# S4 convolution with a gated feed-forward block: the last stage's block loads, one transfer over 128 partitions where there were two over 64

## The chip, the cores and the metric

The kernel runs on one core of one Trainium2 chip. The core has a matrix engine (TensorE, PE in the profile, with its weight loads shown as PEld), three engines for elementwise work (VectorE or DVE, ScalarE or ACT, GpSimd or POOL), a queue that only issues transfers (SyncE, SP) and 16 DMA engines that all the queues share. The metric is the device time of one execution in microseconds. Three runs of the kernel before gave 588.81, 591.67 and 594.80 us.

## What is computed

With L = 2048 tokens, D = 512 channels, N = 128 states per channel and F = 1792 hidden units, all in float32:

```python
x  = A_u                                   # [1, 2048, 512]
xn = layernorm(x)
# s: a long convolution along the tokens, one kernel per channel
P  = exp(dt * A * l)                       # A = A_re + i A_im, l = 0..2047
K  = einsum("dn,dnl,dn->dl", C, P, dt * B).real
s  = irfft(rfft(pad(xn)) * rfft(pad(K)))[:L] + xn * Dskip
# z: a gated feed-forward block
z  = (silu(xn @ w_gate) * (xn @ w_up)) @ w_down
out = x + s * silu(z)
```

## The kernel before

The program is one long list of small tasks. Each call of `add` (L154) makes a task: an engine, a few instructions, the buffers that it reads and writes. `Plan.run` (L190) then emits the tasks in an order that is written out by hand: `LIST` (L46 to L84) is a string in which two characters, base 90, give the number of one task in the order of its making. An engine executes its own tasks strictly in that order. `PLACES` gives each SBUF buffer its place in one tile, the `arena`, so most groups of the profile have the name `arena`; a buffer can be filled when the buffers that lay on its place before are done with. PSUM has eight banks, which `run` hands out (L219 to L226): a product needs its banks free.

Transfers are issued by SP and, for a few of the stores, by ACT. In the program as compiled, the transfers of both queues take eight semaphores in turn, and each one waits, before it is issued, for the transfer eight before it in the program to have landed. A transfer that is issued late on ACT so holds back later ones on SP.

The convolution is done with a transform of three stages over token tiles; the feed-forward block runs on PE in between. The work around the change, in the order of the data:

- `s2_mm`, `s2_prod` (L1282, L1307): for each frequency block n = 0 to 7 and each column half c = 0, 1 (256 channels) PE makes the two products (L1294, L1302) into PSUM banks, DVE multiplies them (L1320, L1322), and POOL combines them into the buffer `y` (L1324, L1325).
- `s2_inv` (L1332): for a pair of blocks m = 0 to 3, PE's inverse product (L1347, 64 matmuls) reads the two `y` and fills four banks. ACT (L1357) and DVE (L1355, L1356) empty each bank into a buffer, and SP stores it to the scratch tensor `bs_d` in DRAM (L1359). `bs_d` has the shape [2, 16, 262, 256]: column half, bank of the inverse product (4m + q), row, column. The stores of the two halves are the keys `bs0` and `bs1`.
- `final(b)` (L1362), for the pairs of token tiles b = 0 to 7: the buffer `bt` (8 KB in each of 128 partitions) takes the blocks from `bs_d`; partitions 0 to 63 hold half 0, partitions 64 to 127 half 1, and e = 0, 1 are the two sets of rows. SP also loads the input `x` in four pieces (L1376, buffer `fx`), and the gate silu(z) from the scratch `zg_d` where it was put there (L1379, pairs 0 to 4). DVE adds the sets (L1386), POOL subtracts them (L1389; DVE for the last pair), PE does the last product (L1401) into two banks, DVE multiplies with the gate (L1418), POOL adds `x` (L1419), and SP and ACT store the output in two pieces each (L1421). The last pair, b = 7, has smaller pieces (L1409, L1410, L1412).
- The feed-forward block runs on beside this until the end: products with `w_gate` and `w_up` (L739, 24 matmuls each), products with `w_down` (`down`, L770: L782, 6 matmuls each; L791 for the last tile), the gate's silu on ACT (L761), L763, L765 and L766 on DVE and ACT, and the silu of the result on ACT (L808 and L803).

The last stage's loads are issued by `load` (L466), so that their issues carry the line L467.

Of the kernel before, what the change touches and what calls it, by code (L numbers as in the profile page):

```python
# [19 lines left out]
P = 128  # L20
L = 2048
D = 512
N = 128
# [15 lines left out]
BN = 2 * P + 6  # L39
# [32 lines left out]
    "3V3N4O3X4v,-,/,05D3Z3U3^4:3O3Y3_3g3e3[3f3i,&3`3b3d,14=4@3a,7,84D55,'473]3c3h3j4F,257,3,44N4P4Q3k4w4E4S4B4R4T3l3m"  # L72
    "3p4V4X3n3q3o3r4x4U4W4Z,(5B4G4I5E4H4K5G5F4y4z4{4Y585:4k4i4J4M594L,),*4|5%5#5$4},+3t3s,?565',@5H5I5K4[4]4c4f5&5J4l"
    "4`,95L5M4m4n4j4^4d4g4a4o4q4p6r6t6u4r5],A6v7#4s5N4u4b,:,;,B4e4_635;5?7%6(5>7&7',N4h,<4t5(5=5<5i645/5051525@53545_"
    "5a5)5*5,5-,O,V5`5A5O,C,D6'5P5Q5+5V5.8<5W655X5R5S5T5Y5Z5[5j6667,H8;688:,J8O6<#*6:698N6;6s,I8M8=6=5k5m,K,L,M6)6*,W"
    "6>6,6+605l6.6-,X6/61,Y5n5p5r5o5q,Z,[6w6{6y5U,P626x,],^5s6?6z6}8P6L6F6G6M,Q5t6@6A6I5^6|7_7$6H7[,i,p6J,q6B6C6D6E5b"
    "5e5f5d5c,R,S,T7(7*7`7+,x6N5g7)7,5h8(6K8)6X,_6P7-,U6Q6O6T6U6R,`6S6W7q7^6Y7r5u6$5v7]6Z6[6]6%7o7W6&5w5x7p5|5},y6#,g"
    "7.6^6a8'6b6`6_6V8*7X-%-&7s5y5z6c5{7/7374797:-',h8s757;7677787071,z726d6e6o6p6q6f6l6i,a6g6h,j,c,l6m,k6n6j6k7l877k"
    ",b,d,e,f7m-(7n7t7u7Z89,r,s,t,m7Y7a,u8&-)8#7v-*,n,o,{8%8$887b7c868+7D7w8,8-7A-+8K8?8@7C8o8L8>-.,|7x8J-C,v8I7F7d7y"
    "7=-,7B--8n7e7f8.8]7h80,}7>8A8C8/7K8q8Q8R7{8p,w7i8^-#-$-/7@7<8[-0-18B8D-2-3-6-4-57G-7818S8U8_7?7z7E7}8F-8-:7J-E-9"  # L80
    "8v8w8x7H8T8V7j-;-<7g7M8E8r7N8t-=8`7L->-?8u838d-@-B7I8a9$7|8X7O8b847Q-A8y8c85828e8W9%8z8|-G8G9'-I-K-M8Z9&9)8H9(7P"
    "8f8h7R7V7S8Y9#-D-F7U8}-O-H-Q7T8g8i8l-J-L8k-N-P8j8m9*8{9+9,9.-R90919-949/939295"
)
LIST = [DIGITS.index(a) * 90 + DIGITS.index(b) for a, b in zip(LIST[::2], LIST[1::2])]  # L84
PLACES = (
# [48 lines left out]
class Plan:  # L134
# [19 lines left out]
    def add(self, eng, dur, fn, rd=(), wr=(), up=(), pr=0.0, c=5, dma=0.0, root=False, port=None, f32=0, slack=0.0, ahead=None):  # L154

        t = Task()  # L160
        t.eng, t.dur, t.fn, t.pr, t.due, t.root, t.seq, t.dma = eng, dur, fn, (c, pr), pr, root, len(self.tasks), dma
        t.after = None
        t.f32, t.slack, t.ahead = f32, slack, W["ah"] if ahead is None else ahead
        t.port = eng == "POOL" if port is None else port
        deps = set()
        for b in rd:
            deps.update(b.full)
            deps.update(b.part)
        for b in up:
            deps.update(b.full)  # L170
            deps.update(b.reads)
        for b in wr:
            deps.update(b.full)
            deps.update(b.part)
            deps.update(b.reads)
        for b in rd:
            b.reads.append(t)
        for b in up:
            b.part.append(t)
        for b in wr:  # L180
            b.full.append(t)
        t.bufs = list(dict.fromkeys(b for b in (*rd, *wr, *up) if b.kind))
        for b in t.bufs:
            b.left += 1
        t.deps = deps
        t.succ = []
        self.tasks.append(t)
        return t
# [118 lines left out]
def dma_us(size, pieces):  # L307
    return max(size / 265e3, pieces * 1.3e-3)
# [73 lines left out]
def kernel(  # L382
# [8 lines left out]
    V, S, G, T = nc.vector, nc.scalar, nc.gpsimd, nc.tensor  # L391
# [10 lines left out]
    def pair(a):  # L402
        return a.rearrange("p (k d) -> p k d", k=2)
# [45 lines left out]
    def buf(name, size, group=None, cap=None):  # L449
        b = pl.buf(name, size, group, cap)  # L450
        bufs.append(b)
        return b
# [6 lines left out]
    K = {}  # L459

    def key(name):
        if name not in K:
            K[name] = pl.key(name)
        return K[name]

    def load(dst, src, names, size, pieces, pr, rd=(), ahead=None):  # L466
        add("SP", 0.52, lambda: sy.dma_start(dst(), src), up=names, rd=rd, pr=pr, dma=dma_us(size, pieces), root=True, ahead=ahead)  # L467
# [859 lines left out]
    def bs_rows(c, n, row, pattern):  # L1327

        v = bs_d[c, n, row]
        return bass.AP(tensor=v.tensor, offset=v.offset, ap=[[a * HD, b] for a, b in pattern] + [[1, HD]])  # L1330
# [31 lines left out]
    def final(b):  # L1362

        j0 = 2 * b
        pr = W["o0"] + W["oc"] + W["o1"] * b
        last = b == NB - 1
        bt = buf(f"bt{j0}", 8192, "bt", int(W["c_bt"] + 0.5))
        btv = lambda: bt.f32().rearrange("p (e s d) -> p e s d", e=2, d=HD)
        for h in range(2):
            for e in range(2):  # L1370
                for first, lo, n in ((0, 0, 1), (33, 1, 1), (2, 2, 2)) if b == 0 else ((2 * j0, 0, 4),):
                    load(lambda h=h, e=e, lo=lo, n=n: btv()[h * 64:(h + 1) * 64, e, lo:lo + n], bs_rows(h, 0, e * P + first, ((BN, 16), (32, 4), (1, n))),
                         [bt], 65536 * n, 64, pr, rd=[key(f"bs{h}")])
        fx = buf(f"fx{j0}", 4096, "fx", int(W["c_fx"] + 0.5))
        for g in range(4):
            add("SP", 0.6, lambda g=g: sy.dma_start(pair(fx.f32()[g * 32:(g + 1) * 32]), rows(xv, b, g)), up=[fx], pr=pr, dma=0.6, root=True)  # L1376
        if b < ZK:
            z = buf(f"fz{j0}", 4096, "fz", int(W["c_fz"] + 0.5))
            load(lambda: pair(z.f32()), zg_d.rearrange("j p d -> p j d")[:, j0:j0 + 2], [z], 524288, 256, pr, rd=[key(f"zgd{j}") for j in (j0, j0 + 1)])  # L1379
        elif not last:  # L1380
            z = zgs[b]
        ev = buf(f"ev{j0}", 4096, "ev", 2)
        od = key(f"od{j0}")

        def even():
            V.tensor_tensor(ev.f32(), bt.f32()[:, 0:1024], bt.f32()[:, 1024:2048], op=ALU.add)  # L1386

        def odd():
            E.tensor_tensor(bt.f32()[:, 0:1024], bt.f32()[:, 0:1024], bt.f32()[:, 1024:2048], op=ALU.subtract)  # L1389
        add("DVE", 1.2, even, rd=[bt], wr=[ev], c=1, pr=pr, port=True)  # L1390
        E = V if last else G
        add("DVE" if last else "POOL", 1.2 if last else 2.05, odd, wr=[bt, od], rd=[ev], c=1, pr=pr, port=True)
        py = [bank(f"py{j0}{h}") for h in range(2)]

        def mm():
            src = [ev.f32().rearrange("p (s d) -> p s d", d=HD), btv()[:, 0]]
            for k in range(2):
                for g, (m, _) in enumerate(at(b)):
                    for h in range(2):
                        r = slice(h * 64, h * 64 + 64)  # L1400
                        T.matmul(py[h].t[g * 32:(g + 1) * 32, k * HD:(k + 1) * HD], j2_t[r, (2 * m + k) * 32:(2 * m + k + 1) * 32], src[k][r, 2 * (g % 2) + m],  # L1401
                                 start=True, stop=True, tile_position=(h * 64, g * 32))
        add("PE", 0.92, mm, rd=[bt, ev, key("j2")], wr=py, c=2, pr=pr, f32=6)
        cols = lambda h: slice(h * HD, (h + 1) * HD)
        if last:
            for k in range(2):
                for h in range(2):
                    o, f = zgs[j0 + k][h], (lambda k=k, h=h: pair(fx.f32())[:, k, cols(h)])
                    add("DVE", 0.42, lambda k=k, h=h, o=o: V.tensor_tensor(o.f32(), py[h].t[:, k * HD:(k + 1) * HD], o.f32(), op=ALU.mult), rd=[py[h]], wr=[o], c=1, pr=pr + 5 * k)  # L1409
                    add("DVE", 0.42, lambda o=o, f=f: V.tensor_tensor(o.f32(), o.f32(), f(), op=ALU.add), rd=[fx], wr=[o], c=1, pr=pr + 5 * k, port=True)  # L1410
                    for g in range(4):
                        add(("SP", "ACT")[g % 2], 0.55, lambda g=g, k=k, h=h, o=o: (sy, nc.scalar)[g % 2].dma_start(rows(ov, b, g)[:, k, cols(h)], o.f32()[g * 32:(g + 1) * 32]),  # L1412
                            rd=[o], up=[key("out")], c=0, dma=0.13, pr=pr + 5 * k)
            return
        zh = {h: key(f"zh{j0}{h}") for h in range(2)}
        for h in range(2):
            zv = lambda h=h: pair(z.f32())[:, :, cols(h)]
            add("DVE", 0.7, lambda h=h, zv=zv: V.tensor_tensor(zv(), py[h].t.rearrange("p (k d) -> p k d", k=2), zv(), op=ALU.mult), rd=[py[h], z], wr=[zh[h]], c=1, pr=pr)  # L1418
        add("POOL", 2.05, lambda: G.tensor_tensor(z.f32(), z.f32(), fx.f32(), op=ALU.add), rd=[fx, zh[0], zh[1]], wr=[z], c=1, pr=pr)  # L1419
        for g in range(4):  # L1420
            add(("SP", "ACT")[g % 2], 0.6, lambda g=g: (sy, nc.scalar)[g % 2].dma_start(rows(ov, b, g), pair(z.f32()[g * 32:(g + 1) * 32])), rd=[z], up=[key("out")], c=0,  # L1421
                dma=0.5, pr=pr)
# [55 lines left out]
    for pos, (b, c) in enumerate(seq):  # L1478
        while pos >= lead(pos) and 2 * NB * NC - len(downs) < 2 * (pos - lead(pos)) + 2:
            d = downs.pop(0)  # L1480
# [18 lines left out]
    for b in range(NB):  # L1499
        final(b)  # L1500
# [13 lines left out]
    for t in order:  # L1514
        n = len(made())
# [35 lines left out]
```

## Time and profile before

| | us |
|---|---|
| median of three runs (588.81 to 594.80) | 591.67 |
| time of the profiled execution | 592.23 |
| its span, from the first to the last instruction | 590.3 |
| PE busy | 563.2 |
| DVE busy | 449.4 |
| POOL busy | 343.4 |
| ACT busy | 332.9 |

The profiled execution's time is 1.93 us more than its span, and 0.56 us above the median. Times in the prediction count from the start of the span unless they are called a run's time. A row of a timeline or of the chain of waits has its start, its length, then engine, line, operation, what it writes and reads, how often, and in brackets the engine's idle time before it with what ended it. A row of "windows" has a stretch, its length, the busy time of PE, PEld, DVE, ACT and POOL with their instructions, then the granted clock of PE, the mean busy share of the DMA engines, and the rate of the transfers.

### The profile page before, as it was taken

To read this page: it belongs to the slowest core of one execution; us is meant where nothing else is said; L and a number is where in the kernel's file an instruction comes from. 1 tells how busy PE (TensorE), PEld (TensorE's weight loads), DVE (VectorE), ACT (ScalarE), POOL (GpSimd) and SP (SyncE) were. 2 spreads that over 40 slices of the span, in tenths; PEclk is the share of its full clock that TensorE was granted. 3 is DMA by queue.
4 is the path that set the end of the run, shared out by engine and by line. 5 is a ranking of instruction groups with operands and counts; after the bars stand their busy time and mean duration, and the time that the engine had idled before them with its cause. 6 is when DMAs were issued, how large, how long until landed. Compare 5 with 4: busy or idle time off the path is not lost.

```text
span 590.3 us, 18770 instructions
## 1 busy us (share of the span) xinstructions
PE 563.2 (95%) x7799; PEld 401.0 (68%) x7799; DVE 449.4 (76%) x1004; ACT 332.9 (56%) x686; POOL 343.4 (58%) x303
## 2 busy tenths in 40 slices
PE   8999999999999999999999999999999999999971
PEld 3888875558884787748866688746755664786541
DVE  7998899467889478899688989778788676548451
ACT  5997786457267367769477778746543412311100
POOL 0154621789279777739976999887163145137541
PEclk9999999999999999999999999999999999999996
DMA  8987722331050143076226474298899889997865
GB/s 237 280 271 273 221 98 40 92 125 38 20 90 2 56 81 100 13 155 211 38 74 108 145 144 74 75 164 263 277 220 290 256 262 256 284 221 203 217 194 157
DMA packets 108373, 93.33 MB, mean 158 GB/s; under 512 B 51520, under 2 KB 88256, under 8 KB 108288
## 3 DMA queue, kind: packets, MB, share of 16 engines
q1 hardware_dynamic: 106480, 89.74, 56.5%
q10 hardware_dynamic: 1808, 2.39, 1.6%
q8 instruction: 61, 1.00, 0.7%
q14 instruction: 24, 0.20, 0.1%
HBM read 56.07 MB, written 32.90 MB: 151 GB/s over the span
## 4 chain that ended last, share of the span: by engine, by line
PE 84%; DMA 9%; SPq 3%; issue 2%; DVE 1%; ACTq 0%; ACT 0%; POOL 0%; DVEq 0%; POOLq 0%
PE p L739 45%; PE p L782 22%; PE p L1208 5%; PE p L1294 3%; DMA out_dram<-arena 3%; PE p L1347 2%; DMA wd<-in_B_w_gate_dram 2%; DMA arena<-zg_d 2%; PE p L1302 2%; PE p L576 2%; PE p L1241 1%; DMA arena<-bs_d 1%; SPq L467 1%; DMA arena<-in_A_u_dram 1%; SPq L494 1%
## 5 line engine op out<-in xcount | busy, mean ns | idle before, releaser
L739 PE MATMUL p<-arena,wg 128*128 128x256 f16 x1344 | 155.1, 273 | 2.5 <-issue 2.5
L739 PE MATMUL p<-arena,wu 128*128 128x256 f16 x1344 | 154.7, 273 | 0.0
L739 PEld LDWEIGHTS <-wg 128*128 128x128 f16 x1344 | 129.7, 98 | 24.9 <-issue 7.9
L782 PE MATMUL p<-wd,arena 128*128 128x512 f16 x630 | 143.4, 379 | 1.6 <-DVE arena L766 1.6
L739 PEld LDWEIGHTS <-wu 128*128 128x128 f16 x1344 | 130.5, 98 | 19.4 <-issue 3.2
L782 PEld LDWEIGHTS <-arena 128*128 128x128 f16 x630 | 59.4, 98 | 75.9 <-issue 9.1
L1141 POOL TENSOR_TENSOR arena<-arena 128x1536 f32<-128x1536 f32 x32 | 90.6, 2839 | 11.0 <-DVE arena L1254 3.7
L1133 POOL TENSOR_TENSOR arena<-arena 128x1024 int32<-128x1024 int32 x32 | 62.3, 1955 | 22.2 <-ACT arena L811 11.6
L761 ACT ACTIVATE arena<-p,inv 128x512 f32<-128x512 f32 x56 | 38.1, 687 | 62.1 <-PE p L739 59.1
L763 DVE SCALAR_TENSOR_TENSOR p<-p,shc,arena 128x512 f32<-128x512 f32 x56 | 42.0, 754 | 21.8 <-PE p L739 20.0
L765 ACT CAST arena<-p 128x512 f16<-128x512 f32 x56 | 32.3, 589 | 46.6 <-DVE p L763 36.3
L1176 DVE TENSOR_TENSOR arena<-arena,p 128x512 f32<-128x512 f32 x64 | 43.5, 679 | 8.3 <-POOL arena L1141 4.6
L1158 ACT ACTIVATE p<-arena 128x512 f32<-128x512 int32 x64 | 37.9, 600 | 9.3 <-POOL arena L1133 7.2
L766 DVE TENSOR_TENSOR arena<-p,arena 128x512 f16<-128x512 f32 x56 | 37.6, 682 | 6.5 <-ACT arena L765 6.5
L1157 ACT ACTIVATE p<-p,halfpi 128x512 f32<-128x512 f32 x64 | 41.8, 659 | 1.0
L1156 ACT ACTIVATE p<-arena 128x512 f32<-128x512 int32 x64 | 38.1, 604 | 4.9 <-POOL arena L1133 2.4
L1324 POOL TENSOR_TENSOR arena<-arena 128x512 f32<-128x512 f32 x16 | 20.4, 1276 | 29.4 <-issue 16.0
L1325 POOL TENSOR_TENSOR arena<-arena 128x512 f32<-128x512 f32 x16 | 20.3, 1273 | 26.0 <-DVE arena L1320 14.7
L1208 PEld LDWEIGHTS p<-arena 128*32 128x32 f32 x2048 | 29.5, 110 | 6.3 <-issue 5.0
L1208 PE MATMUL p<-arena 128*32 128x64 f32 x2048 | 32.1, 220 | 1.3 <-issue 1.3
L1389 POOL TENSOR_TENSOR arena<-arena 128x1024 f32<-128x1024 f32 x7 | 16.5, 2356 | 28.2 <-DVE arena L1386 25.0
L1182 DVE SCALAR_TENSOR_TENSOR arena<-arena,p 128x256 f32<-128x256 f32 x64 | 26.4, 412 | 5.8 <-PE p L1208 2.0
(197 smaller groups left out, 823.0 us busy)
## 6 DMA issues: line engine op xcount, KB each, us to landing
ax_d<-arena SPq DMA_DIRECT2D x32, 256.0 KB, 3.3
ak_d<-arena SPq DMA_DIRECT2D x16, 512.0 KB, 5.5
arena<-ak_d SPq DMA_DIRECT2D x16, 512.0 KB, 5.3
arena<-ax_d SPq DMA_DIRECT2D x16, 512.0 KB, 5.4
bs_d<-arena SPq DMA_DIRECT2D x32, 256.0 KB, 4.0
arena<-in_A_u_dram SPq DMA_DIRECT2D x62, 128.0 KB, 3.7
arena<-in_B_w_down_dram SPq DMA_DIRECT2D x14, 512.0 KB, 5.8
arena<-bs_d SPq DMA_DIRECT2D x28, 256.0 KB, 5.7
```

The costliest lines, as they stand in the source:

```text
L739: T.matmul(pg.t[:, i * 256:(i + 1) * 256].rearrange("p (a t) -> p a t", a=2), w[:, wl, d, i * P:(i + 1) * P], x[:, :, xl, d, :], start=(k ...
L761: add("ACT", 0.69, lambda: S.activation(sg.f32(), pg.t, AF.Silu, scale=inv[:, c, 0:1]), rd=[pg, *([key("inv0")] if c == 0 else [])], wr=[s ...
L763: add("DVE", 0.75, lambda: V.scalar_tensor_tensor(pu.t, pu.t, shc[:, c:c + 1], sg.f32(), op0=ALU.mult, op1=ALU.mult), rd=[sg], wr=[pu], c= ...
L766: add("DVE", 0.7, lambda: V.tensor_tensor(hh.view(F16)[:, 512:1024], pu.t, hh.view(F16)[:, 0:512], op=ALU.subtract), rd=[pu], wr=[hh], c=1 ...
L782: T.matmul(z.t, h[:, hl, i * 256 + t * P:i * 256 + (t + 1) * P], w[:, wl, i], start=(c == 0 and i == 0 and k == 0), stop=(c == NC - 1 and ...
L1133: G.tensor_tensor(a, h_[:, :, :, None].to_broadcast([P, 2 * GT, 4, 8]), l_[:, :, None, :].to_broadcast([P, 2 * GT, 4, 8]), op=ALU.add)
L1141: G.tensor_tensor(e, p_[:, :, :, None].to_broadcast([P, 3 * GT, 4, 8]), q_[:, :, None, :].to_broadcast([P, 3 * GT, 4, 8]), op=ALU.mult)
L1156: add("ACT", 0.62, lambda: S.activation(tc_.t, a(), AF.Abs, scale=SIN_SCALE), rd=[an], wr=[tc_], pr=pr)
L1157: add("ACT", 0.7, lambda: S.activation(tc_.t, tc_.t, AF.Sin, bias=halfpi, scale=-1.0), rd=[key("ones")], wr=[tc_], c=4, pr=pr)
L1158: add("ACT", 0.62, lambda: S.activation(ts.t, a(), AF.Sin, scale=SIN_SCALE), rd=[an], wr=[ts], pr=pr + 0.2)
L1176: V.tensor_tensor(o[:, :, 0:64].rearrange("p d (s j) -> p d s j", s=2), e[:, :, 0:64].rearrange("p d (s j) -> p d s j", s=2), t[:, :, None ...
L1208: T.matmul(kt[h * 32:(h + 1) * 32, (r * GD + dd) // 4], o[:, ri, dd + h, 64:96], o[:, ri, dd + h, 0:64], start=(ri == 0), stop=(ri == 1), ...
```

## The change

For each pair b and each e there was one load for each column half: partitions h·64 to h·64+63, 64 rows of up to 4 KB. Now there is one load that covers all 128 partitions. The half's blocks lie one behind the other in `bs_d`, so the pattern (262, 16) over half 0 and the same over half 1 become (262, 32). Pairs 1 to 7 have two loads of 512 KB where they had four of 256 KB. Pair 0, whose rows lie in three places, has six (128 KB or 256 KB) where it had twelve (64 KB or 128 KB). 40 loads become 20, with the same bytes. Each load now waits for the stores of both halves.

```diff
-        for h in range(2):
-            for e in range(2):
-                for first, lo, n in ((0, 0, 1), (33, 1, 1), (2, 2, 2)) if b == 0 else ((2 * j0, 0, 4),):
-                    load(lambda h=h, e=e, lo=lo, n=n: btv()[h * 64:(h + 1) * 64, e, lo:lo + n], bs_rows(h, 0, e * P + first, ((BN, 16), (32, 4), (1, n))),
-                         [bt], 65536 * n, 64, pr, rd=[key(f"bs{h}")])
+        for e in range(2):
+            for first, lo, n in ((0, 0, 1), (33, 1, 1), (2, 2, 2)) if b == 0 else ((2 * j0, 0, 4),):
+                load(lambda e=e, lo=lo, n=n: btv()[:, e, lo:lo + n], bs_rows(0, 0, e * P + first, ((BN, 32), (32, 4), (1, n))),
+                     [bt], 131072 * n, 128, pr, rd=[key(f"bs{h}") for h in range(2)])
```

The rest of the diff is the end of `LIST`, since 20 tasks are gone and the others are numbered anew. `PLACES` stays. Decoded, the new order differs in these places and no others:

| queue | before | after |
|---|---|---|
| PE | L1302 (n=5, c=1), **two L782 of tile 13**, L1347 (m=3), **L739 gate**, L1347 (m=2), L739 gate, L739 gate, ... | L1302 (n=5, c=1), L1347 (m=3), L1347 (m=2), **two L782 of tile 13**, **L739 gate**, L739 gate, L739 gate, ... |
| ACT | two L1357, two L808 (tiles 13, 12), six L1357 | eight L1357, two L808 |
| SP | two loads of half 0 for pair 1 and the gate of pair 2 and one L1376 of pair 7 stand between the stores of half 1 | these come after the last store of half 1, and the 20 loads follow in the order of pairs 1, 2, 2, 4, 1, 3, 3, 4, (gate 3), 0, 5, (gate 4), 5, 0, 0, 7, 7, 6, 0, 0, 6, 0 with the same `x` loads and output stores between them |
| DVE, POOL | | the same order |

Here tile 13 is the second of pair b = 6, and the three products of the PE row are the last tile pair's, b = 7. The block n = 5 is one of the two that the inverse product m = 2 reads.

More of the change, by code (lines that the diff above doesn't have):

```diff
@@ L74 @@
     "4`,95L5M4m4n4j4^4d4g4a4o4q4p6r6t6u4r5],A6v7#4s5N4u4b,:,;,B4e4_635;5?7%6(5>7&7',N4h,<4t5(5=5<5i645/5051525@53545_"
[L75 to L82, printed above, removed]
+    "5a5)5*5,5-,O,V5`5A5O,C,D6'5P5Q5+5V5.8.5W655X5R5S5T5Y5Z5[5j6667,H8-688,,J8?6<#*6:698>6;6s,I8=8/6=5k5m,K,L,M6)6*,W"
+    "6>6,6+605l6.6-,X6/61,Y5n5p5r5o5q,Z,[6w6{6y5U,P626x,],^5s6?6z6}8@6L6F6G6M,Q5t6@6A6I5^6|7V7$6H7S,i,p6J,q6B6C6D6E5b"
+    "5e5f5d5c,R,S,T7(7*7W7+,x6N5g7)7,5h7w6K7x6X,_6P7-,U6Q6O6T6U6R,`6S6W7g7U6Y7h5u6$5v7T6Z6[6]6%7e6&5w5x7f5|5},y6#,g7."
+    "6^6a7v6b6`6_6V7y5y5z5{7/737475797:7;7677787071726c6d6e6o6p6q6f6g6h6l6m6n6i6j6k7Q-%-&7i-',h8_,z,a,j,c,l,k7c,b,d,e"
+    ",f-(7d7j7k8*,r,s,t,m7R7X,u-)7t7l-*,n,o,{7u7Y7Z8+7z7m7{7|7<-+81828;80-.,|7n-C,v8<7=7[7o-,7>--8[7]7^7}7`8$,}83858#"
+    "7E8A8B7q8],w7a8K-#-$-/7?-0-18486-2-3-6-4-57@-78%8C8E8L7p7A7s88-8-:7D-E-98b8c8d7B8D8F7b-;-<7_7G878^7H8`-=8M7F->-?"
+    "8a8'8Q-@-B7C8N8k7r8H7I8O8(7K-A8e8P8)8&8R8G8l8f8h-G898n-I-K-M8J8m8p8:8o7J8S8U7L7P7M8I8j-D-F7O8i-O-H-Q7N8T8V8Y-J-L"
+    "8X-N-P8W8Z8q8g8r8s8u-R8w8x8t8{8v8z8y8|"
 )
```

## Prediction

> **What bounds the kernel now.** I read the page first, for the share of each engine, then the end of the chain of waits, the timelines of PE, DVE, POOL and ACT from 499 us on, the waits of SP, and stretches for the rates.
>
> ```profile
> span 590.3 us, 18770 instructions
> PE 563.2 (95%) x7799; PEld 401.0 (68%) x7799; DVE 449.4 (76%) x1004; ACT 332.9 (56%) x686; POOL 343.4 (58%) x303
> 508.57:578.01 69.44, 62.99 (x699) 46.06 (x694) 37.10 (x50) 10.90 (x21) 30.44 (x13) 1.00 0.84 215
> ```
>
> PE is the bound of the whole. The last stage, from 508.57 on, is looser: PE stands 69.44 - 62.99 = 6.45 us before its last matmul ends at 578.0, and 12.3 us follow in which it does nothing. A change here can return those 6.45 us and a part of the 12.3, and no more. What makes PE stand, and what makes the tail:
>
> ```profile
> 563.35 1.04 PE L782 MATMUL p<-wd,arena 128*128 128x512 f16 x4 [1.63 <-DVE arena L766]
> 571.01 1.09 PE L1401 MATMUL p<-arena,j_t 64*32 64x256 f32 x30 [1.88 <-DVE arena L1418]
> 572.60 5.40 PE L791 MATMUL p<-wd,arena 128*128 128x256 f16 x48 [0.51 <-DVE arena L1418]
> 570.26 0.69 DVE L1418 TENSOR_TENSOR arena<-p,arena 128x512 f32<-128x512 f32 x1 [3.72 <-DMA arena<-zg_d]
> 578.47 2.34 POOL L1419 TENSOR_TENSOR arena<-arena 128x1024 f32<-128x1024 f32 x1 [3.35 <-DMA out_dram<-arena]
> 582.23 0.47 ACT L803 ACTIVATE arena<-p,zsc 128x256 f32<-128x256 f32 x1 [4.78 <-issue]
> ```
>
> DVE waits 3.72 us for the gate of pair 0; behind it stand the release of the banks that PE wants at 571.01 and the last pair's L1409 and L1410. POOL's L1419 of pair 6 waits for that pair's last piece of `x`; ACT's queue holds its two stores, and behind them the last L803. That is how 12.3 us come about.
>
> The late loads have one cause, SP's queue:
>
> ```profile
> SPq L467 <- DMA out_dram<-arena: 6.5, 1, 6.5
> 545.71 2.43 SPq L467 DMA_DIRECT2D arena<-bs_d  x4
> 564.98 0.53 SPq L467 DMA_DIRECT2D arena<-zg_d  x1
> 575.42 0.57 SPq L1376 DMA_DIRECT2D arena<-in_A_u_dram  x1
> SPq L1421 <- DMA out_dram<-arena: 2.1, 1, 2.1
> ```
>
> SP stands 6.5 us until an output store of ACT's has landed (545.7; one of the eight semaphores). From 545.71 to the gate at 564.98 it issues 24 transfers in 19.3 us: 14.6 us of issues at 0.61 us each, as in the row at 545.71 (2.43 / 4), and 4.6 us of shorter waits. It is bound mostly by its issues. The last piece of `x` at 575.42 again waits for a store of ACT's to land, the one issued at 572.39. The last row is a wait among SP's own last stores, from 583.1 to 585.2.
>
> **The change part by part.**
>
> *The rate of a load.*
>
> ```profile
> 520.00:525.00 5.00, 5.00 (x48) 4.49 (x47) 1.90 (x2) 0.49 (x1) 1.86 (x1) 1.00 1.03 201
> 12.00:26.00 14.00, 13.30 (x146) 9.82 (x145) 13.63 (x39) 13.51 (x25) 1.90 (x1) 1.00 0.99 319
> 540.00:545.00 5.00, 5.00 (x43) 4.08 (x42) 3.11 (x5) 0.33 (x1) 3.56 (x3) 1.00 0.40 86
> ```
>
> Loads over 64 partitions alone fill the DMA engines (1.03) at 201 GB/s; the first loads of weights, over 128, fill them (0.99) at 319. No row shows a 4 KB row over 128 partitions, so the rate lies between 201 (no gain) and 319; I take 319, the row with the same partitions. The loads are 28 x 262144 + 4 x 131072 + 8 x 65536 = 8.4 MB: 41.7 us of DMA time become 26.3, a saving of 15.4. But at 540 to 545 the engines are idle to 60%: SP waits, not the data. So I cost the rate itself at 0; its cover is that the first blocks, which would land some 4 us sooner, meet a later PE (next part).
>
> *The new order on PE.* Before:
>
> ```profile
> 499.66 0.71 PE L1302 MATMUL p<-arena 32*32 32x256 f32 x32
> 500.30 2.76 PE L782 MATMUL p<-wd,arena 128*128 128x512 f16 x12
> 503.00 1.50 PE L1347 MATMUL p<-arena 32*32 32x256 f32 x64
> 504.42 2.79 PE L739 MATMUL p<-arena,wg 128*128 128x256 f16 x24
> 507.15 1.49 PE L1347 MATMUL p<-arena 32*32 32x256 f32 x64
> 500.42 0.69 DVE L1320 TENSOR_TENSOR arena<-p,arena 128x512 f32<-128x512 f32 x1 [1.05 <-DMA bs_d<-arena]
> 502.23 0.68 DVE L1320 TENSOR_TENSOR arena<-p,arena 128x512 f32<-128x512 f32 x1
> 504.27 1.27 POOL L1325 TENSOR_TENSOR arena<-arena 128x512 f32<-128x512 f32 x1
> 504.80 0.42 DVE L1355 TENSOR_TENSOR arena<-p,arena 128x256 f32<-128x256 f32 x1 [1.10 <-ACT arena L1357]
> 508.57 5.41 PE L739 MATMUL p<-arena,wg 128*128 128x256 f16 x48
> ```
>
> The second L1347 reads `y` of block 5, which is made from the L1302 at 499.66 by DVE until 502.91 and by POOL until 504.27 + 1.27 = 505.54. Before, 2.70 us of L782, the first L1347 and 2.73 us of L739 cover that chain. After, only the first L1347 (1.42) stands between, and the cover is gone. At the least, PE ends the second L1347 at 505.6 + 1.42 = 507.0, then does 2.70 + 2.73, and reaches the point of 508.57 at 512.4: +3.9 us. Banks may cost more: the two feed-forward sums are no longer emptied in between, so the first L1347 waits until DVE has read the banks of L1302 (502.9 at the latest), and the second for two pairs of L1355 and L1356 after it (504.80 + 2 x 0.8 = 506.4): 506.4 + 1.42 + 5.43 = 513.3, +4.7. I take +4.4, nearer the upper end since six of eight banks are held. The last store of half 1 (now at 512.5) goes out after the second L1347, about 1 us sooner than now, and no merged load can start before it has landed. The rows are the stores' and the loads':
>
> ```profile
> L1359 SPq DMA_DIRECT2D bs_d<-arena x8: 359/360/452, 505.7 to 512.5; - x8
> DMA to landing us min/median/max: 2.3/3.1/4.0
> 512.92 10.40 SPq L467 DMA_DIRECT2D arena<-bs_d  x14
> ```
>
> 511.5 + 2.3 = 513.8 against 512.92: the first loads start 0.9 us later. The two loads of pair 1, the gate of pair 2 and the `x` piece that are moved behind the stores start some 10 to 18 us later. Both cost nothing, since the product that first needs a block (L1401 of pair 2, now at 527.02) moves to 531.4, and the loads land by about 522; without that cover each would cost its delay.
>
> *The clock.* The hole, 505.6 - 500.4 less the 1.42 of work, is 3.8 us and more.
>
> ```profile
> 576.70:580.10 3.40, 1.30 (x12) 0.92 (x10) 0.85 (x2) 0.47 (x1) 1.64 (x1) 1.00 0.86 253
> 580.20:586.00 5.80, 0.00 (x0) 0.00 (x0) 0.85 (x2) 0.47 (x1) 0.60 (x1) 0.50 0.64 170
> ```
>
> After a stretch of 3.4 us with 1.30 us of matmuls the granted clock went to 0.50. The hole has stretches of that length with 1.0 to 1.4 us of work, so the clock may halve for one: 3.4 / 2 = 1.7 us. Bounds 0 and +1.7; I take 0, because gaps of up to 1.88 us (571.01) left it at 1.00, and keep 1.7 for a rival. [...]
>
> *Where PE's idle time goes.* With blocks and gates in time none of the 6.45 us remains: PE ends at 578.0 + 4.4 - 6.45 = 576.0. Until 550 little speeds up, since DVE, POOL and SP follow PE: the loads of pairs 0 and 5 and the gate of pair 4 wait for places that L1386, L1389 and L1401 of earlier pairs leave.
>
> ```profile
> 538.51 4.68 POOL L1419 TENSOR_TENSOR arena<-arena 128x1024 f32<-128x1024 f32 x2
> PE p L791 <- DVE arena L1418: 1.4, 2, 0.9
> PE p L1401 <- DVE arena L1386: 0.8, 1, 0.8
> PE p L1401 <- DVE arena L1389: 0.5, 1, 0.5
> ```
>
> The first ACT store, whose landing frees SP at 545.7, follows these two L1419. They follow L1389 of pair 4, that follows L1386 of pair 4, and on DVE that one stands behind an L763 that waits for PE. PE's product for it ends at 530.8, and then at 535.2. L763 (0.75), L1386 (1.2 to 2.7), L1389 (2.35) and 4.68 give 544.2 to 545.7; the store lands 2.5 later (as from 543.2 to 545.7). I take 547.5 for SP, +1.8.
>
> *SP's queue after that.* Of the 24 issues up to the gate, 14 are block loads; they become 8, and 18 issues remain if the wait falls on the same load. 547.5 + 18 x 0.61 = 558.5 without any other wait, 547.5 + 18 x 19.3 / 24 = 562.0 with as many as now. I take 561 for the gate's issue (now 564.98), nearer the upper end, because the semaphores go on making waits. It lands 5.2 later, at 566.2; the row is the gate's:
>
> ```profile
> DMA to landing us min/median/max: 5.2/5.2/5.2
> 566.13 0.41 DVE L1409 TENSOR_TENSOR arena<-p,arena 128x256 f32<-128x256 f32 x1
> 568.33 0.56 SPq L1376 DMA_DIRECT2D arena<-in_A_u_dram  x1
> 572.39 1.26 ACTq L1412
> ```
>
> L1409 follows the silu of what PE's L782 at 563.35 ends; this comes at +4.4 less the gaps up to there (0.9 + 0.8 + 0.5 + 1.63 = 3.8), so 0.6 us later, and L1409 at 566.7. The gate is there, the 3.72 us are gone, and the last pair's first stores go out at 572.39 + 0.6 - 3.72 = 569.3.
>
> *What is late next.* SP's L1376 at 568.33 waits for an ACT store behind an L803, which comes 0.6 us later too, but SP's own way there is shorter: I leave it where it is. Its landing, 3.2 us on, releases a store at 571.7, and the last piece of `x`, which needs the store of 569.3 to have landed (+3.0), follows at 572.3 and not at 575.42: -3.1. POOL's L1419, ACT's two stores and the last L803 (582.23) follow it. Behind L803 there are 590.3 - 582.23 = 8.1 us of L1409, L1410, eight small stores and their landing, unchanged.
>
> *Sum.* 590.3 - 3.1 = 587.2 us of span. The profiled run took 1.93 us more than its span and lay 0.56 above the median of 591.67: 587.2 + 1.93 - 0.56 = **588.6 us**, 0.5% less. A measurement of this kernel can tell about 1% from no change.
>
> **The rivals.**
>
> *The stage is bound by its transfers, and they get faster.* For it: DMA share 1.03 at 201 GB/s, and 15.4 us to save. Against it: the share of 0.40 at 540, and SP's 0.61 us per issue. If every wait on SP goes, the last L803 is free when PE ends (576.0), and the end comes 8.1 us later, less the 2.1 us that SP waits among its last stores, at 582.0: a time of **583.4**. [...]
>
> *The loads are hidden anyway.* SP's order of stores stays, and each waits for ACT's and POOL's pace. If the gate is held until a store that PE's later course delays, the tail moves by the +0.6 only: 590.9, a time of **592.3**. Against it: three quarters of SP's time between 545.7 and 565 are issues.
>
> *Slower: the hole on PE is not given back.* Its place is the second L1347, its price +4.4, and +1.7 if the clock falls. If the gate and the pieces of `x` come no sooner, the end is 590.3 + 6.1 = 596.4, a time of **597.8**. It decides from the point at which less than 0.2 us of the 6.1 is absorbed in PE's 6.45 us of waiting. Against it: L766 and L1418, for which PE waited, have their inputs sooner.
>
> **How the numbers follow.** My forecast 0.50 (its own range 585.5 to 591: the hole 3.9 to 4.7, the gate's issue 558.5 to 562, and the spread of the runs), the faster transfers 0.24, hidden 0.13, the hole kept 0.13. Faster by over 1%, under 585.8: the second and the lower edge of the first, 0.27. Slower by over 1%, over 597.6: nearly all of the last, 0.12. Within 1%: 0.61. The range from 582.8 to 594.5 leaves out the last case and the lower part of the second, 0.18.
>
> **What would show it.** PE's timeline with a hole of about 4 us before the second L1347, and the point of 508.57 at 512.4 to 513.3. Loads from `bs_d` 20 times 512 KB or less, and over 300 GB/s where they fill the engines. DVE's L1418 without its 3.72 us. L803 at about 579. Wrong: a hole under 3 us, a gate later than 564, a granted clock under 1 near 505, or an end that PE's last matmul, and no longer SP's or ACT's queue, sets.

## The result, and the profile after

| | before | after |
|---|---|---|
| median of 14 runs each, us | 590.78 | 585.86 |
| lowest to highest, us | 588.81 to 594.80 | 583.28 to 589.03 |
| time of the profiled execution | 592.23 | 586.04 |
| its span | 590.3 | 584.0 |
| its last matmul ends | 578.0 | 574.6 |
| from there to the end | 12.3 | 9.4 |

The ratio is 0.9921, with a 95% interval of 0.9898 to 0.9943: 0.8% faster, 4.9 us between the medians. The ratios in this document are estimated from the fast runs of both kernels (one run of the kernel before, at 605.8 us, was slow and is left out) and are not quotients of the medians. The two profiled executions lie 6.2 us apart, since the one of before stood 1.45 us above its median. In the traces 3.4 us of this come off PE's end and 2.9 off the stretch behind it. Of the 3.4, 0.9 us stand already at the L1302 from which the order differs, which starts at 498.75 and started at 499.66; in the twelve profiled executions of this document that start lies anywhere between 497.8 and 501.7.

In what follows the lines of `final` in the changed kernel are one lower than before: L1400 is the product that was L1401, L1375 the load of `x`, L1385, L1388 and L1417 were L1386, L1389 and L1418, and L1411 and L1420 are the stores. First the chain that ended last in the kernel before, then two lines of the page of the changed kernel: busy times, and its chain.

```profile
PE 84%; DMA 9%; SPq 3%; issue 2%; DVE 1%; ACTq 0%; ACT 0%; POOL 0%; DVEq 0%; POOLq 0%
PE 565.2 (97%) x7799; PEld 402.6 (69%) x7799; DVE 450.2 (77%) x1004; ACT 333.4 (57%) x686; POOL 343.4 (59%) x303
PE 87%; DMA 6%; DVE 2%; issue 2%; SPq 1%; ACTq 0%; ACT 0%; POOL 0%; DVEq 0%
```

PE holds more of the chain than before, and is busy 2.0 us longer, though its work is the same: a part of "busy" is waiting, or work at a lower clock. PE's timeline at the place of the new order:

```profile
498.75 0.73 PE L1302 MATMUL p<-arena 32*32 32x256 f32 x32
499.18 0.85 PE L1347 MATMUL p<-arena 32*32 32x256 f32 x8
500.25 2.60 PE L1347 MATMUL p<-arena 32*32 32x256 f32 x60 [0.22 <-DVE arena L1320]
503.45 3.22 PE L1347 MATMUL p<-arena 32*32 32x256 f32 x60 [0.61 <-POOL arena L1324]
506.61 4.31 PE L782 MATMUL p<-wd,arena 128*128 128x512 f16 x12
510.76 8.03 PE L739 MATMUL p<-arena,wg 128*128 128x256 f16 x72
```

The idle time in brackets is only 0.22 and 0.61 us. But 60 of these matmuls take 2.60 and 3.22 us here, where 64 took 1.50 before, and 12 of L782 take 4.31 instead of 2.76. Of the 72 in the last row the first 24 are the gate product that moved, so the point called 508.57 in the prediction lies near 513.4: 14.7 us behind the start of L1302 against 8.9 before, a hole of 5.8 us. The windows show the granted clock there:

```profile
499.55:502.96 3.41, 3.08 (x68) 1.03 (x60) 3.38 (x7) 0.55 (x2) 0.84 (x1) 1.00 0.52 165
502.97:506.38 3.41, 2.93 (x60) 1.50 (x60) 2.83 (x8) 0.73 (x3) 1.65 (x2) 0.50 0.79 259
506.38:509.79 3.41, 3.41 (x12) 1.18 (x9) 2.52 (x7) 1.20 (x4) 0.00 (x0) 0.50 0.62 202
513.50:574.62 61.12, 61.11 (x695) 46.12 (x692) 35.28 (x43) 9.70 (x17) 32.85 (x14) 1.00 0.76 245
```

The clock was at 0.50 from 502.97 to 509.79, 6.8 us. The row at 500.25 is long at a clock of 1.00, so it holds waiting. From 513.5 to its last matmul PE then never stops, while before it stood still several times up to 1.88 us. The loads are the other half. Two windows while they fill the DMA engines:

```profile
517.00:522.00 5.00, 5.00 (x48) 4.47 (x46) 0.49 (x1) 1.26 (x2) 0.00 (x0) 1.00 1.03 359
522.00:527.00 5.00, 5.00 (x48) 4.48 (x46) 3.47 (x5) 0.58 (x1) 1.70 (x1) 1.00 1.02 406
```

359 and 406 GB/s at a share of 1.02 to 1.03, against 201 at 1.03 before. The last rows are SP's issues of the gate of pair 0 and of two late pieces of `x`, the product on DVE that had waited for that gate, and ACT's last silu:

```profile
560.41 0.53 SPq L467 DMA_DIRECT2D arena<-zg_d  x1
565.26 0.57 SPq L1375 DMA_DIRECT2D arena<-in_A_u_dram  x1
567.65 1.39 SPq L1375 DMA_DIRECT2D arena<-in_A_u_dram  x1
565.68 0.69 DVE L1417 TENSOR_TENSOR arena<-p,arena 128x512 f32<-128x512 f32 x1 [0.22 <-PE p L1400]
575.00 0.47 ACT L803 ACTIVATE arena<-p,zsc 128x256 f32<-128x256 f32 x1 [2.24 <-DMA out_dram<-arena]
```

(SPq is SP's queue.) The gate is issued 4.57 us sooner than before, DVE's wait of 3.72 us for it is gone (0.22, and for PE), and the last L803 comes 7.23 us sooner.

### The profile page after: what moved, and what is told of

Same layout as the page of the kernel before. It is cut to its first block, busy times and chain, and to the rows that moved or that the text cites. A ratio compares the mean times of both kernels' runs of the same rounds, so it can differ in the third digit from the quotient of the medians.

```text
span 584.0 us, 18736 instructions
## 1 busy us (share of the span) xinstructions
PE 565.2 (97%) x7799; PEld 402.6 (69%) x7799; DVE 450.2 (77%) x1004; ACT 333.4 (57%) x686; POOL 343.4 (59%) x303
## 4 chain that ended last, share of the span: by engine, by line
PE 87%; DMA 6%; DVE 2%; issue 2%; SPq 1%; ACTq 0%; ACT 0%; POOL 0%; DVEq 0%
PE p L739 49%; PE p L782 22%; PE p L1208 5%; PE p L1294 3%; PE p L1347 2%; PE p L576 2%; PE p L1241 1%; DMA arena<-ak_d 1%; PE p L1302 1%; DMA arena<-in_A_u_dram 1%; DMA arena<-ax_d 1%; DMA bs_d<-arena 1%; PE p L1400 1%; DMA out_dram<-arena 1%; PE p L857 1%
## 5 line engine op out<-in xcount | busy, mean ns | idle before, releaser
L739 PE MATMUL p<-arena,wg 128*128 128x256 f16 x1344 | 154.9, 273 | 2.3 <-issue 2.3
L739 PE MATMUL p<-arena,wu 128*128 128x256 f16 x1344 | 154.7, 273 | 0.0
L739 PEld LDWEIGHTS <-wg 128*128 128x128 f16 x1344 | 129.7, 98 | 24.3 <-issue 6.8
L782 PE MATMUL p<-wd,arena 128*128 128x512 f16 x630 | 144.8, 383 | 0.0
L739 PEld LDWEIGHTS <-wu 128*128 128x128 f16 x1344 | 130.4, 98 | 19.6 <-issue 3.2
L782 PEld LDWEIGHTS <-arena 128*128 128x128 f16 x630 | 59.9, 98 | 75.5 <-issue 11.6
L766 DVE TENSOR_TENSOR arena<-p,arena 128x512 f16<-128x512 f32 x56 | 37.7, 683 | 6.8 <-ACT arena L765 6.7
L1388 POOL TENSOR_TENSOR arena<-arena 128x1024 f32<-128x1024 f32 x7 | 16.5, 2355 | 30.9 <-DVE arena L1385 28.2
```

The costliest lines, as they stand in the source:

```text
L739: T.matmul(pg.t[:, i * 256:(i + 1) * 256].rearrange("p (a t) -> p a t", a=2), w[:, wl, d, i * P:(i + 1) * P], x[:, :, xl, d, :], start=(k ...
L766: add("DVE", 0.7, lambda: V.tensor_tensor(hh.view(F16)[:, 512:1024], pu.t, hh.view(F16)[:, 0:512], op=ALU.subtract), rd=[pu], wr=[hh], c=1 ...
L782: T.matmul(z.t, h[:, hl, i * 256 + t * P:i * 256 + (t + 1) * P], w[:, wl, i], start=(c == 0 and i == 0 and k == 0), stop=(c == NC - 1 and ...
```

## The experiments

The change has two parts, merged loads and a new order. My theory A was that the gain is the transfers' rate, that the new order costs a part of it, and that the cost is the hole on PE. Rivals were that the new order is free (its waits being given back), and that the smaller number of issues on SP, not the rate, is the gain. Each run was timed beside the kernel before on the same chip; that had medians of 590.41, 591.95 and 591.59 us in the three groups below. In a run whose edit adds lines the line numbers are up to 14 higher: in the first, L1315 is L1302, L1360 is L1347 and L752 is L739.

**The old order with the merged loads.** The tasks of PE and ACT in the order's table go back to where they stood. The loads stay as changed, and so does SP's order: the loads still come after the last store of half 1.

```diff
+def move(tasks, before):
+    for t in tasks:
+        LIST.remove(t)
+    i = LIST.index(before)
+    LIST[i:i] = tasks
+move([902, 903], 1812)
+move([904, 878], 1819)
+move([896], 1773)
```

> The merged loads stay, but PE and ACT get back their order of before: the two L782 ahead of the first L1347, the L739 ahead of the second, the two L808 in their old place. Theory A (the time comes from the loads; the new order on PE takes 5.7 us of it back, by waits and a halved clock between 500 and 510): no hole and no clock under 1 near 505, PE reaches the last pair's first gate product at about 508.6 and not at 513.4, the span falls from 584.0 to 579 to 582, ratio to the kernel before 0.981 to 0.987. Theory B (the new order is what gains, since the last store of half 1 goes out sooner; the hole costs nothing because PE would only wait later): ratio 0.992 or above, and waits of 5 us on PE come back behind 510.

Measured: 583.85 us, ratio 0.9874 [0.9851, 0.9897]. PE's timeline:

```profile
499.22 0.71 PE L1315 MATMUL p<-arena 32*32 32x256 f32 x32
499.87 2.76 PE L795 MATMUL p<-wd,arena 128*128 128x512 f16 x12
502.56 1.49 PE L1360 MATMUL p<-arena 32*32 32x256 f32 x64
503.99 2.79 PE L752 MATMUL p<-arena,wg 128*128 128x256 f16 x24
506.71 1.49 PE L1360 MATMUL p<-arena 32*32 32x256 f32 x64
508.14 5.41 PE L752 MATMUL p<-arena,wg 128*128 128x256 f16 x48
...
526.49 3.62 PE L1515 MATMUL p<-ones 128*128 128x512 bf16 x16
```

The two inverse products take 1.49 us each again, the clock stays at 1.00 (from 498 to 515), and the point of 508.57 is back at 8.9 us behind the start of that L1302. So the order costs PE time; ratio and span (582.2) lie just above what A allowed. The last row was not expected. The program's planner (`keep_warm`, L270) puts products of a matrix of ones where it reckons PE idle; in the last stage of the kernels before and after it puts none, but with this mixture it put 16, which take 3.6 us. They are taken up below.

**The new order with the old rate.** Each load is issued as two over 64 partitions.

```diff
-                load(lambda e=e, lo=lo, n=n: btv()[:, e, lo:lo + n], bs_rows(0, 0, e * P + first, ((BN, 32), (32, 4), (1, n))),
-                     [bt], 131072 * n, 128, pr, rd=[key(f"bs{h}") for h in range(2)])
+                def halves(e=e, first=first, lo=lo, n=n):
+                    for h in range(2):
+                        sy.dma_start(btv()[h * 64:(h + 1) * 64, e, lo:lo + n], bs_rows(h, 0, e * P + first, ((BN, 16), (32, 4), (1, n))))
+                add("SP", 0.52, halves, up=[bt], rd=[key(f"bs{h}") for h in range(2)], pr=pr, dma=dma_us(131072 * n, 128), root=True)
```

> The new order stays, but each load is issued as two transfers over 64 partitions, 40 in all as before. Theory A: DMA rate near 200 GB/s again between 515 and 530, SP has 20 issues more, PE has the hole and waits behind it as well, span 590 to 595, ratio 0.998 to 1.010. Theory B: ratio 0.990 to 0.994, as with merged loads.

Measured: 594.5 us, ratio 1.0067 [1.0045, 1.0089]. One window, and then rows of the timelines of DVE and PE:

```profile
522.00:527.00 5.00, 5.00 (x49) 4.49 (x47) 2.58 (x3) 0.59 (x1) 0.00 (x0) 1.00 1.06 236
```

```profile
558.68 1.23 DVE L1387 TENSOR_TENSOR arena<-arena 128x1024 f32<-128x1024 f32 x1 [3.56 <-DMA arena<-bs_d]
568.38 1.23 DVE L1387 TENSOR_TENSOR arena<-arena 128x1024 f32<-128x1024 f32 x1 [5.94 <-DMA arena<-bs_d]
569.52 0.69 DVE L766 TENSOR_TENSOR arena<-p,arena 128x512 f16<-128x512 f32 x1
...
570.26 1.89 PE L782 MATMUL p<-wd,arena 128*128 128x512 f16 x4 [5.24 <-DVE arena L766]
```

This is how a late load reaches PE: the sum of the sets (here L1387) waits 5.94 us on DVE for its block, L766 of the feed-forward block stands behind it in DVE's queue, and PE's product waits 5.24 us for L766. During that wait the granted clock falls a second time: its mean from 567 to 572 is 0.62, which fits 0.50 from 568.2 on, and the 4 of L782 take 1.89 us, where 4 took 1.04 in the kernel before at a clock of 1.00 (563.35). The gate of pair 0 is issued only at 570.60. The profiled execution, 596.65 us, was the slowest of six.

**The new order, full rate, more issues.** The larger loads are again two transfers each, but each over 128 partitions with half of every partition's bytes (2 KB in a row for pairs 1 to 7): 36 issues. The lines with a minus are the same as in the edit before.

```diff
+                def rows2(e=e, first=first, lo=lo, n=n):
+                    m = max(n // 2, 1)
+                    for k in range(0, n, m):
+                        sy.dma_start(btv()[:, e, lo + k:lo + k + m], bs_rows(0, 0, e * P + first + k, ((BN, 32), (32, 4), (1, m))))
+                add("SP", 0.52, rows2, up=[bt], rd=[key(f"bs{h}") for h in range(2)], pr=pr, dma=dma_us(131072 * n, 128), root=True)
```

> The new order stays; each load is issued as two transfers over 128 partitions with half the rows each (36 in all, 2 KB rows). This keeps the rate and undoes nearly all of the saving in issues. If the number of issues on SP is what counts: the gate of pair 0 goes out 3 us later, span 586 to 589, ratio 0.995 to 1.000. If the rate is what counts: within 1 us of the changed kernel, ratio 0.990 to 0.994.

Measured: 587.37 us, ratio 0.9930 [0.9903, 0.9957], as the changed kernel. The same window as above:

```profile
522.00:527.00 5.00, 5.00 (x48) 4.49 (x47) 3.43 (x5) 0.59 (x1) 1.25 (x1) 1.00 1.05 390
```

36 issues or 20 make 0.1% of difference, less than the intervals tell apart; 236 or 390 GB/s make 1.4%, and those intervals lie apart. The gate of pair 0 is issued at 561.95, and at 560.41 with 20 issues; it lands late enough that DVE waits 2.6 us for it, in the slowest of this run's seven executions. So the rate is the gain as far as these runs can tell, and what 16 more issues cost is too small for them. With the kernel before, these runs make a square of four:

| ratio | 64 partitions a load | 128 partitions a load |
|---|---|---|
| old order | 1 (before) | 0.9874 |
| new order | 1.0067 | 0.9921 (after) |

In the lower row only the loads differ: they bring 1.5%. In the right column only the order of PE and ACT differs: it costs 0.5%. The upper row (1.3%) and the left column (0.7%) hold SP's new order as well, since the run of the old order has it and the kernel before has not; what SP's order is worth alone was not tried. The 0.5% rests on the changed kernel's first 14 runs. Its repeat below gives 0.9891, only 0.2% from the old order, with intervals that overlap, so the order's cost is seen more surely in PE's timelines than in the times.

**Two products back alone.** Only the two products L782 stand again between L1302 and the first inverse product: `move([902, 903], 1812)`.

> The merged loads stay; of the order only the two L782 go back ahead of the first L1347. Theory A: waits of 1 to 2 us are left before the second L1347, the clock stays at 1.00 or halves for one stretch, span 580.5 to 583, ratio 0.984 to 0.990. Theory B: ratio 0.992 or above.

Measured: 585.09 us, ratio 0.9906 [0.9877, 0.9934], just above what A gave and below what B gave. In the profile the 72 gate matmuls behind gaps of 0.72 and 0.16 us take 8.03 us, as the 72 at 510.76 in the changed kernel do at a clock of 1.00. The mean clock of this execution is 0.996, and the last matmul ends at 571.55; this execution's time, 582.66, was the lowest of six. 8 fillers had been put in. This run alone does not separate from the changed kernel.

**One gate product back alone**, between the two inverse products: `move([878], 1819)` and `move([896], 1773)`. The second is the product; the first is one L808 on ACT, the silu of an earlier tile's result, and no step of that product. With it, in the same group, ran a version with another tail, and the changed kernel again.

> The merged loads and the changed order, with one gate product alone (task 896, 24 matmuls) put back between the last two inverses, and its scalar step (878) with it; the two products of the output projection stay behind. Theory A (what the new order costs is the hole ahead of the second inverse and the halved clock behind it, and any work of full size in that place removes both): no gap over 0.3 us at the second inverse, granted clock 1.00 from 499 to 514, ratio 0.985 to 0.990, as with the whole old order (0.9874). Rival B (the hole only moves: the first inverse waits instead, or the clock falls anyway): ratio 0.990 to 0.995, as the changed kernel (0.9921).

> The changed kernel itself, beside the other two on the same chip: ratio 0.990 to 0.994 as in its first runs; granted clock halved between about 503 and 510 in most of its profiles.

Measured: 584.68 us, ratio 0.9880 [0.9849, 0.9911], and the changed kernel beside it 585.69, 0.9891 [0.9862, 0.9920], a little lower than in its first runs (0.9921). The latter's profile has the halved clock again, 0.53 on average from 502.70 to 509.50. PE of the former:

```profile
500.55 2.49 PE L1359 MATMUL p<-arena 32*32 32x256 f32 x56 [0.22 <-DVE arena L1332]
502.97 2.79 PE L751 MATMUL p<-arena,wg 128*128 128x256 f16 x24
505.69 1.49 PE L1359 MATMUL p<-arena 32*32 32x256 f32 x64
```

The hole ahead of the second inverse product and the halved clock are gone, as A said (the rows have their length at 1.00, and the execution's mean clock is 0.996), but the ratios are too near to tell; this order too had fillers, 8 of them.

**The tail.** The last tile's four stores of SP go to ACT: `("SP", "ACT")[k or g % 2]` in place of `[g % 2]`, for the issue and its queue alike, in the old order with merged loads. `move([1969, 1971], 1970)` puts two of the four behind the last L803, so that they do not hold it up on ACT.

> The merged loads in the old order (as in the first experiment, ratio 0.9874, 9.4 us from the last matmul to the end), with the last token tile's four stores that SP issued given to ACT, which is idle by then. Theory A (the end is set by SP's issue of output stores, four of about 0.4 us each at its end, and by no engine of arithmetic): the end comes 0.8 to 1.8 us sooner, ratio 0.9840 to 0.9862, with the last matmul where it was (572.8). Rival B (the landing or the last product sets the end): ratio 0.9865 to 0.989, as without it.

Measured: 583.94 us, ratio 0.9867 [0.9839, 0.9894]. A's bound was missed, narrowly, and the interval holds A's values too. SP has its last issue at 577.77, after these waits:

```profile
SPq L1434 <- DMA out_dram<-arena: 2.2, 3, 1.4
SPq L1425 <- DMA out_dram<-arena: 2.0, 2, 1.8
```

From 568 on SP waits 4.2 us for output stores to land, where it waits 2.7 in the first experiment. The stretch from the last matmul to the end is 9.2 us, and was 9.4: giving SP fewer issues hardly shortened it. What sets it stays open.

**Without the fillers.** `if s > 480 or max(idle...` in `keep_warm` skips the gaps of the last stage, in three of these orders.

> The merged loads in the old order, without the 16 filler matmuls (products of a matrix of ones that the program's planner puts where it reckons PE idle; 3.6 us at 526.5 in the first experiment, none in the changed kernel, whose result nobody reads). Theory A (the fillers stood on PE's path, so the old order is better than the first experiment showed): no gap over 1.5 us at 526, the last matmul 1.5 to 3.5 us sooner than 572.8, ratio 0.981 to 0.985. Rival B (they stood in a wait for pair 2's blocks, or the tail is set by other queues): a gap of 2 us or more at 526, or the same end; ratio 0.986 to 0.990.

> One gate product put back between the last two inverses, without the 8 filler matmuls (1.9 us at 528) that this order got. Theory A: the last matmul 1 to 1.8 us sooner than 572.7, ratio 0.982 to 0.987. Rival B: the same end as with them, ratio 0.987 to 0.990.

> The merged loads in the old order without fillers, and the last token tile's stores all on ACT. If PE's end and SP's issue of stores both count, 0.5 to 1.5 us under the run without fillers alone: ratio 0.979 to 0.984. If the landings of the stores set the end, the same as that run to 0.001.

Measured: the old order 583.72 us, ratio 0.9874 [0.9841, 0.9907]; the gate product back 583.04, 0.9853 [0.9830, 0.9876]; the old order with the other tail 583.44, 0.9870 [0.9844, 0.9896]. For the first and the last the ratio did not move, as the rivals had it. For the last that was to mean that the landings of the stores set the end, which these runs do not show by themselves. The old order's PE shows what the fillers had covered (the gap is smaller than rival B's 2 us; the last matmul comes 0.8 us sooner, at 572.0):

```profile
526.60 0.66 PE L1413 MATMUL p<-arena,j_t 64*32 64x256 f32 x16
528.91 0.67 PE L1413 MATMUL p<-arena,j_t 64*32 64x256 f32 x16 [1.64 <-POOL arena L1401]
```

The old order brings PE to pair 2's product before the block is through DVE and POOL, so it waits there instead. The order with one gate product back does not, and theory A's ratio held, though the interval reaches the rival's lower bound of 0.987. Its last matmul, at 570.1, came 2.6 us sooner than 572.7, more than A said; counted from the start of L1302 it is 1.7. PE's timeline:

```profile
502.05 2.79 PE L751 MATMUL p<-arena,wg 128*128 128x256 f16 x24
504.78 1.50 PE L1359 MATMUL p<-arena 32*32 32x256 f32 x64
508.81 5.40 PE L751 MATMUL p<-arena,wg 128*128 128x256 f16 x48
527.24 1.09 PE L1412 MATMUL p<-arena,j_t 64*32 64x256 f32 x32
```

It has neither the hole nor the wait. From the start of L1302 to the last matmul the profiled executions need:

| | us |
|---|---|
| before | 78.3 |
| after | 75.9 (again: 76.1) |
| old order, merged loads | 73.6, without fillers 72.8, without fillers and with the other tail 73.5 |
| one gate product back | 73.6, without fillers 71.9 |

The two runs of the old order without fillers give PE the same work and differ by 0.7 us, so that much is spread between executions, and what the 16 fillers cost is not told from it. The hole ahead of the second inverse product and the halved clock cost PE about 3.9 us in the changed kernel (75.9 - 71.9), well beyond that. The version with one gate product back and no fillers is faster than the kernel before. Its interval lies below that of the changed kernel's first 14 runs and overlaps that of its 6 later ones (0.9862 to 0.9920), so that it beats the changed kernel is likely and not shown.

## Why the prediction came out right, step by step

The predicted 588.6 us was 2.7 above the measured 585.86, and the span 587.2 was 3.2 above 584.0. That the change is a little faster was right, with the mechanism partly another. That the number lay so near was in part luck: what the faster loads give was put at 0, the hole and the clock were put too low, and these errors point opposite ways. Without the rate the new order is slower than the kernel before, 594.5 us.

- **Rate, costed at 0.** This is the step that failed. The loads did reach 359 to 406 GB/s, but I took their 15.4 us of DMA time as covered, since PE came later and SP's queue had waits of its own. At the old rate in the new order the kernel takes 594.5 us, 8.6 more than the changed one. The rival that let the transfers count put 0.24 on this, and was right about the cause; it left out the cost of the order, 0.2 to 0.5% against the 1.5% that the loads bring.
- **SP's queue.** The gate's issue at 561 (560.41) and its landing at 566.2 (565.25) were right by luck, since the reason was not: I worked it out from 14 issues becoming 8. With 36 loads at full rate it is issued at 561.95, with 40 at the old rate at 570.60.
- **The new order, +4.4.** The mechanism was right, its size was not: 5.8 us. The waits that I worked out are there, partly inside long rows of matmuls: with one gate product back the same point lies 1.8 us later than before, from the first inverse product, and the hole ahead of the second and the clock add 4.0.
- **The clock, taken at 0.** It was at 0.50 for 6.8 us, for which 0 to 1.7 was allowed; the 1.7, half of one stretch of 3.4 us, was the author's estimate, and the traces showed no such stretch but the 6.8. By another estimate from these rows the 6.8 us cost at most half of that, 3.4 us: the 12 of L782 from 506.61 take 4.31 us, 3.18 of them at 0.50, and 3.18 / 2 + 1.13 = 2.72 is about the 2.76 that they took before at 1.00. Part of the 3.4 would have been waiting anyway, and what the clock alone costs was not separated. Among the 14 runs of the changed kernel the only one with a mean clock of 0.996 had a span of 581.2, the others, at 0.989 to 0.990, 582.4 to 587.0. In the run with 36 loads the two executions with 0.995 and 0.996 were the fastest of seven, 583.69 and 584.82 us.
- **PE's idle time given back, 6.45.** 8.3 came back: from the point of 508.57 on PE needed 69.4 us before and 61.1 after. My sum of gaps left out that a wait in the middle of a group of matmuls costs more than the gap shown: 32 of the final product take 1.09 us in one piece, and 0.66 and 0.67 where a wait parts them (564.32 and 565.18 before). The same 256 matmuls, before and after:

```profile
L1401 PE MATMUL p<-arena,j_t 64*32 64x256 f32 x256 | 9.8, 383 | 3.4 <-DVE arena L1418 1.9 <-DVE arena L1386 0.8 <-DVE arena L1389 0.5
L1400 PE MATMUL p<-arena,j_t 64*32 64x256 f32 x256 | 8.5, 382 | 0.0
```

  The "busy" time fell by 1.3 us for the same work. PE's end, 576.0 in the sum, came at 574.6: the larger hole added 1.4 us, the waits gave back 1.9 more than the 6.45, and 0.9 was there before the changed place.
- **The tail.** The piece of `x` that I left at 568.33 went out at 565.26, right when the gate had landed, for which SP waits 1.8 us there, and the last piece at 567.65 instead of 572.3. The last L803 came at 575.0 and not at 579: the 4.0 us of it are more than the whole error of the span. From there to the end it took 9.0 us and not 8.1.
- **What would make it wrong.** The granted clock under 1 near 505 came true, and stretched the hole; it did not turn the result, because the faster loads gave more.

What makes the clock fall was not shown. In the 3.41 us from 499.55, just before the fall, PE ran 68 matmuls, which need about 1.6 us back to back (64 take 1.49), and is shown busy for 3.08; the idle times shown are 0.22 and 0.61 us. The clock falls and returns only once there.

## What to carry to other kernels

When a change makes transfers faster and also moves work, measure the four combinations: here the loads brought 1.5%, and the order that came with them took up to 0.5% back. See that each of the four differs from its neighbour in one thing only; here SP's order slipped in between two of them. A late block need not hold PE by itself; look for what stands behind its consumer in the next engine's queue, as L766 stood behind the sum of the sets. And compare the busy time of one group of matmuls in two places before adding up gaps, because part of a wait also lies inside rows that the profile calls busy (9.8 us here for 256 matmuls with waits between them, 8.5 without).

## What the hardware showed that was not expected

- The clock was halved, at 0.50 for 6.8 us, with no idle time above 0.61 us shown on PE, after a window in which it is shown busy for 3.08 of 3.41 us, on matmuls that need about 1.6. With 24 large matmuls in that place (2.79 us) it was at 1.00 from 500 to 510 (the gate product back, without fillers). The fall came in all four profiles with the whole new order (a mean clock of 0.52, 0.52 and 0.55 from 503 to 510, and in the repeat 0.53 from 502.70 to 509.50), and in none of the eight that had large matmuls between the two inverse products or ahead of them: five of these show 1.00 there, and in the other three the gate matmuls have their length at 1.00 (24 in 2.79 us, 72 in 8.03).
- Loads over 128 partitions reached 406 GB/s with rows of 4 KB and 390 with rows of 2 KB, each in its fullest window (359 and 304 in the window before); over 64 partitions the engines were as full (share 1.06) at 236, with 271 in the window before.
- Cutting the number of loads from 36 to 20, at nearly the same rate, changed the time by 0.1%, within the intervals.
